# A new stored table of places and engines for a fused attention and gated MLP kernel

## The chip, the core and the metric

The kernel runs as one program on one core of a Trainium2 chip. The metric is the device time in microseconds (us) of one execution; before the change its median is 655.58 us over 3 runs (651.97 to 656.78).

The core has five instruction queues that run side by side and wait for one another through semaphores: PE (matrix products), DVE (vector), ACT (activations), POOL (the general engine) and SP (here: issues the DMAs). Each works through its own queue strictly in order.

## The reference

```python
# attention, 8 batches x 8 heads, 576 positions, 64 wide
scores = (1/8) * q @ k.T
psi = log1p(|i - j|) / log1p(max(i, 1))
bias = relu(psi * w1 + b1) @ w2          # (576, 576, 8 heads), the same for all batches
attn = softmax(scores + bias) @ v
# gated MLP on x = heads side by side, (8, 576, 512)
gate = sigmoid(causal_conv(x, conv_w))   # 5 taps for each of 512 channels
out  = (gate * (x @ w_val)) @ w_out
```

The inputs are float32. Where the kernel multiplies in 16 bits it splits an operand into a high and a low half and adds up two or three products, and it divides by the softmax's sum only after the product with v.

## The kernel before

**The parts.** `bias_rows` (L294) builds the bias once, 16 rows of positions at a time in 36 pieces: ramps on ACT, DVE and POOL, a product on PE, then a copy to SBUF and a store to DRAM in a skewed layout, from which `bias_ld` loads it back for each pair of heads. `weight` brings the two weight matrices into 16-bit halves. `pair(n)` (L603) is attention for two heads of one batch, 32 of them; `mlp(b)` (L1096) is the gated MLP of one batch, 8 of them, whose work lies among that of the pairs after it. The MLP of the last batch has only the end of the kernel to lie in.

**One pair.** For each of four blocks of 128 rows (and a fifth, `c` = 4, of the 64 remaining rows of two pairs): `qkm` on PE makes the scores of both heads (8 products, tile t_sp, L704); `logits` on DVE adds the bias and finds the row's extreme (L750); `expo` on ACT takes the exponential (L762). In 24 of the 32 pairs ("split" pairs) the exponentials are then split: `top` casts them to 16 bits (ACT L194, POOL L198 or DVE L196), `rest` subtracts that from the original for 2 x 512 columns and `rest8` for the last 2 x 64 (POOL or DVE, L217), and `swap` transposes both halves by a DMA issued on SP (L943). The other 8 pairs normalise first (`norm`, L824 or L212) and transpose on PE (`tp`, L909, with copies `tev`). `piece` (L976) multiplies with v: five groups for each half g of the 512 rows; `rem_mm` (L1050) does the remaining rows; `ev` and `mu` (L1033, L1075) bring the result to SBUF. v itself is scaled and split by `vinv` (L658), `vhi` (L212) and `vlo` (L205).

**One MLP.** Taps of the convolution run on DVE through PSUM (L1173) or, for the last channels and the last batch, as products on ACT or POOL (`prod`, L1133, L1135) and sums on DVE or POOL (`acc`, L1138) or both in one on DVE (`conv`, L1123); `sig` is the gate on ACT (L1186). x is split into halves (`split_hi`, `split_lo`). `val` (L1241) multiplies with w_val in two parts of 256 and 320 positions and four groups d of channels, three products q each; `gf` (L1251) applies the gate on DVE; `ghi` and `glo` (L194, L196, L198 and L217) split the result; `outp` (L1307) multiplies with w_out; `ote` scales the rows out of PSUM (L1319 on ACT, L201 on DVE) and a DMA stores them.

**What sets the order.** The functions do not issue at once. Each `add(...)` makes a step (a `Task`): the engines that could run it, the function that issues it, and the steps it depends on. There are 4,041 steps. The table `ORDER` (L46 on) is the only thing that decides the sequence. Unpacked, it holds two bytes for each step, which `Plan.order` (L114) reads as step number and engine:

```python
        for lo, hi in zip(code[:n], code[n:]):
            t = self.tasks[(lo + 256 * hi) // 4]
            assert not t.done and all(d.done for d in t.deps)
            t.on, t.done = t.engines[lo % 4], True
...
    for t in plan.order():
        t.fn(t.on)
```

The steps are issued in the table's order, so each engine's queue is the table's subsequence for that engine, and buffers of the rings (4 PSUM banks for products, 2 transposed halves, 2 of q and k, 7 and 13 larger SBUF buffers) go to whoever takes them next in that order. Dependencies and the waits they need are worked out from the program as issued. The other figures in the code (due times such as `PAIR_AT`, costs in `add`) are not used when a stored table is there.

Of the kernel before, what the change touches and what calls it, by code (L numbers as in the profile page):

```python
# [1479 lines left out]
```

## Time and profile before

| | |
|---|---|
| median of 3 runs | 655.58 us (651.97 to 656.78) |
| the profiled execution | 653.45 us |
| its span, first to last instruction | 651.6 us, so 1.85 us lie outside it |
| PE busy | 617.4 us (95%), 6,176 products |
| DVE, ACT, POOL busy | 590.3, 571.9, 520.3 us (91%, 88%, 80%) |
| granted TensorE clock | 0.997 over the span |

The trace is of one execution. "Busy" is the time in which an engine has an instruction under way; the ends of PE's pipelined products are modelled, so a busy PE can still hide some waiting. The views used further on are the totals by engine, the same in four stretches of the span, the chain of work that ended last (followed back from the last instruction to what released each step), the waits, the groups of like instructions, and the timeline of single instructions.

### The profile page before, as it was taken

The page shows a single profiled execution, that of the slowest core. Times are in us where ns is not written, and L with a number is a line of the kernel's source. Part 1 is how long each engine was busy: PE and PEld are TensorE (multiplying, and loading weights), DVE is VectorE, ACT ScalarE, POOL GpSimd, SP SyncE. Part 2 cuts the span into 40 slices and gives each one's busy share as a digit, 9 for nine tenths or more (in the row PEclk, how much of TensorE's full clock was granted, in tenths as well). Part 3 has the DMA queues.
Part 4 walks back from the last instruction along what each step waited for, and adds up shares of the span by engine and source line. Part 5 has one row for each costly group of instructions (what it writes and reads, how often), then busy time and mean ns, then how long its engine had stood idle before and what let it go on. Part 6 is the DMA issues. An engine that isn't in the chain of part 4 may idle for free.

```text
span 651.6 us, 16872 instructions
## 1 busy us (share of the span) xinstructions
PE 617.4 (95%) x6176; PEld 398.0 (61%) x6176; DVE 590.3 (91%) x1575; ACT 571.9 (88%) x1284; POOL 520.3 (80%) x585
## 2 busy tenths in 40 slices
PE   6777999999899999999999999899999999999997
PEld 2223667766566666667666665666676666766663
DVE  7999999999999988898998989899989889999982
ACT  6898999999999998999789989989979998899561
POOL 5889858687797988997798989787979787898441
PEclk9989999999999999999999999999999999999999
DMA  7888885246999999999999999999964999999712
GB/s 243 274 280 283 277 307 177 82 136 126 236 160 218 207 225 207 210 199 226 206 234 225 212 230 193 211 216 198 222 162 125 179 200 195 221 201 184 133 66 81
DMA packets 279107, 129.77 MB, mean 199 GB/s; under 512 B 255600, under 2 KB 255856, under 8 KB 279024
## 3 DMA queue, kind: packets, MB, share of 16 engines
q1 hardware_dynamic: 278880, 128.40, 89.3%
q8 instruction: 48, 0.79, 0.5%
q14 instruction: 35, 0.29, 0.2%
q10 hardware_dynamic: 144, 0.29, 0.1%
HBM read 44.64 MB, written 20.33 MB: 100 GB/s over the span
## 4 chain that ended last, share of the span: by engine, by line
PE 54%; DVE 10%; POOL 10%; DMA 8%; ACT 6%; issue 3%; SPq 0%; POOLq 0%; DVEq 0%; ACTq 0%
PE t_sp L704 14%; PE t_ps L976 11%; PE t_ps L1307 9%; PE t_ps L1241 9%; DMA t_pt<-t_d 6%; POOL t_d L217 5%; PE t_ps L909 5%; DVE t_d L750 4%; ACT t_d L762 3%; DMA t_d<-t_d 2%; PE t_sp L720 2%; ACT t_d L194 2%; PE t_ps L1050 1%; PE t_ps L1029 1%; POOL t_d L198 1%
## 5 line engine op out<-in xcount | busy, mean ns | idle before, releaser
L217 POOL TENSOR_TENSOR t_d<-t_d,t_d 128x1024 f16<-128x1024 f32 (+1 forms) x180 | 245.4, 1383 | 32.8 <-ACT t_d L194 23.8
L762 ACT ACTIVATE t_d<-t_d,nm 128x576 f32<-128x576 f32 x288 | 222.2, 774 | 17.6 <-DVE nm L750 17.0
L750 DVE CUSTOM_DVE_ANT_0 t_d<-t_sp,bias 128x576 f32<-128x576 f32 x256 | 184.8, 751 | 22.7 <-PE t_sp L704 12.5
L704 PE MATMUL t_sp<-t_qk 64*128 64x288 f32 x1024 | 165.1, 429 | 1.7 <-DVE nm L750 1.2
L976 PE MATMUL t_ps<-t_pt,t_w 128*64 128x256 f16 (+1 forms) x1664 | 124.1, 296 | 7.0 <-DMA t_pt<-t_d 5.1
L704 PEld LDWEIGHTS t_sp<-t_qk 64*128 64x128 f32 x1024 | 92.6, 186 | 48.2 <-DVE nm L750 12.4
L194 ACT CAST t_d<-t_d 128x576 f16<-128x576 f32 x157 | 100.5, 668 | 7.8 <-DMA t_pt<-t_d 3.3
L1241 PEld LDWEIGHTS <-wv 128*128 128x128 f16 x768 | 72.6, 98 | 31.7 <-issue 12.4
L976 PEld LDWEIGHTS <-t_w 128*64 128x64 f16 x1344 | 69.7, 110 | 23.3 <-issue 14.0
L1241 PE MATMUL t_ps<-xh,wv 128*128 128x256 f16 (+1 forms) x480 | 69.2, 285 | 0.1
L1173 DVE SCALAR_TENSOR_TENSOR t_ps<-t_xp,convw,t_ps 128x288 f32<-128x288 f32 x126 | 64.3, 516 | 1.5 <-ACT t_ps L1164 0.8
L1307 PE MATMUL t_ps<-wo,gh 128*128 128x512 f16 x240 | 57.7, 380 | 0.0
L762 ACT ACTIVATION_READ_ACCUMULATOR t_d<-t_d,nm 128x1 f32 x288 | 56.0, 194 | 0.0
L337 PE MATMUL t_ps<-rel,w 128*32 128x272 f32 (+17 forms) x352 | 42.9, 520 | 12.2 <-ACT t_be L356 3.8
L318 POOL TENSOR_SCALAR rel<-gt,ip,nb 128x336 f32<-128x336 f32 (+14 forms) x21 | 47.1, 2248 | 8.4 <-PE t_ps L337 8.0
L824 POOL TENSOR_SCALAR t_d<-t_d,rinv 128x576 f32<-128x576 f32 x57 | 45.0, 799 | 8.9 <-DVE rinv L796 8.5
L318 DVE TENSOR_SCALAR rel<-gt,ip,nb 128x368 f32<-128x368 f32 (+17 forms) x87 | 46.5, 591 | 1.6 <-PE t_ps L337 1.6
L198 POOL TENSOR_SCALAR t_d<-t_d 128x576 f16<-128x576 f32 x49 | 35.4, 724 | 14.9 <-ACT t_d L762 7.0
L909 PE MATMUL t_ps<-ident,t_d 128*128 128x128 f32 x324 | 43.2, 278 | 0.8 <-DVE vsc L648 0.4
L909 PEld LDWEIGHTS t_ps<-ident,t_d 128*128 128x128 f32 x324 | 35.1, 140 | 14.0 <-issue 7.1
L1307 PEld LDWEIGHTS <-gh 128*128 128x128 f16 x240 | 22.1, 98 | 27.5 <-issue 4.8
L1241 PE MATMUL t_ps<-xl,wv 128*128 128x256 f16 (+1 forms) x240 | 38.0, 285 | 0.4 <-DVE xl L205 0.4
(159 smaller groups left out, 1088.6 us busy)
## 6 DMA issues: line engine op xcount, KB each, us to landing
t_qk<-qkd SPq DMA_DIRECT2D x32, 576.0 KB, 4.7
bias_d<-t_be SPq DMA_DIRECT2D x36, 295.5 KB, 4.5
bias<-bias_d SPq DMA_DIRECT2D x16, 576.0 KB, 6.5
out<-t_w SPq DMA_DIRECT2D x32, 256.0 KB, 3.0
t_w<-vd SPq DMA_DIRECT2D x24, 320.0 KB, 3.9
t_w<-vn SPq DMA_DIRECT2D x8, 320.0 KB, 4.3
t_d<-wod SPq DMA_DIRECT2D x4, 512.0 KB, 5.0
t_d<-wvd SPq DMA_DIRECT2D x4, 512.0 KB, 5.3
```

Of the source, the lines that this page charges most:

```text
L194: A.copy(out=out, in_=in_)
L217: (V if e == "V" else G).tensor_tensor(out=out, in0=in0, in1=in1, op=ALU.subtract)
L318: (G if e == "G" else V).tensor_scalar(out=rel[g].t[:, 0:w], in0=src, scalar1=sct[:, mm : mm + 1], scalar2=nb1, op0=ALU.mult, op1=ALU.max,)
L704: T.matmul(ts[a][:, j, 0:hw], lhsT=qk.t[r, c * P : (c + 1) * P], rhs=qk.t[r, x : x + hw], start=True, stop=True,)
L750: V.tensor_tensor_reduce(out=part(c, a).rearrange("p (j f) -> p j f", j=2), in0=sp.t[:, :, 0 : S // 2], in1=bias.rearrange("p (j f) -> p j ...
L762: A.activation(out=part(c, a), in_=part(c, a), func=AF.Exp, bias=nms[c][:, a : a + 1], scale=-1.0, accum_out=sums[c][:, a, 0:1],)
L824: (G if e == "G" else V).tensor_scalar(out=t, in0=t, scalar1=rinvs[c][:, a : a + 1], scalar2=1.0, op0=ALU.mult, op1=ALU.mult,)
L909: T.transpose(t[:, k * P : (k + 1) * P], es[c].t[:, (k0 + k) * P : (k0 + k + 1) * P], ident)
L976: T.matmul(po.t[r, 0:256], lhsT=vt.t[:, v, r], rhs=pt[:, x, :, :] if tr else pt[:, :, x, :], start=(t == 0 and m == 0), stop=(t == 4 and m ...
L1173: V.scalar_tensor_tensor(out=o, in0=x, scalar=wt, in1=t, op0=ALU.mult, op1=ALU.add)
L1241: T.matmul(pm.t[:, 0:w], lhsT=weights["wv"][wi][:, k, d * P : (d + 1) * P], rhs=xb.t[xi][:, k, 0:w], start=(q == 0 and k == 0), stop=(q == ...
L1307: T.matmul(pm.t, lhsT=gb.t[gi][:, k, o : o + P] if o < 256 else gx.t[gi][:, k, :], rhs=weights["wo"][wi][:, k, :], start=(q == 0 and k == ...
```

## The change

Only the lines of `ORDER` differ. Its origin is stated as a search for the mean over runs in which every step of three engines is shaken widely. The 4,041 steps, what each computes and what each depends on stay as they are. 97 steps run on another engine than before, and within each queue many steps stand a few places earlier or later. Two of the table's lines stand here, the first of the old and the first of the new:

```diff
 ORDER = (
-    'c-nPW4`?#!nfJ>#nn^NACUML+NhZl8ndBRjNgR_&GD#*|TinAv{J<?1+~O7&+`}F&xWz5*Vh?**u;3OKT(HF+F1X+p_prsUxQBbV;8*P7ci3XVf(5_g9`4~D7TjVFx7_oN`T7s;aprlSKfmYqyz}RMC&69fyoU66-4x~v(*8iG-cXuSi>on>I?LxSA6l$7d%Ica<Xfdk^!Zpkk#75J<w`Qs^LK;JK&bDqyPou9ELpErSlk&Fx`W{e52qsT'
...
+    'c-mc84`?d+oj31I%p{p4lQ<@mWRgshNix1n;+TxdB$>S0;vR1Cfm<xN#Vszlhdo?yi#=?a9u{2iz!rPBU=Q!GV8Jae*y1bh;T|ryhdq3U1q&AJ;THF>hkJNni#=?)?{9ps*WTCPpYNZ~_w)PBZ|3)#5%-8oIv?rxDijt7(~V%L9^n|4&)+<4wxnje(P`Q24rj5@ZI`35_$!G{AenJgs;O*0)N{Fm;mE-0>3_`1SW0bF1zb%JN8@PR+xNNa'
...
 )
```

By kind, the steps that change engine and that the prediction speaks of:

| step | moves |
|---|---|
| `rest8` | 9 from DVE to POOL |
| `glo` | 7 from DVE to POOL, 4 from POOL to DVE |
| `ghi` | 5 DVE to ACT, 2 ACT to DVE, 4 POOL to ACT, 3 ACT to POOL |
| `top` | 5 POOL to ACT, 1 DVE to ACT, 1 ACT to POOL, 1 ACT to DVE, 1 POOL to DVE |
| `tev` | 4 (of 512 columns) DVE to ACT, 1 (of 128) ACT to DVE |
| `ote` | 5 DVE to ACT, 3 ACT to DVE |
| `vlo`, `vhi` | 1 DVE to POOL, 1 ACT to POOL |
| `acc` | 1 POOL to DVE (in the last MLP) |
| steps of a few columns, and single others | 38 |

**First place: POOL in the last pair.** POOL's queue before, from a half for the second-last MLP to the last `rest8`. `x2x64` is a `rest8` of a pair, `rhl`, `rinvs` and `bsc` are small steps, `gh` and `gl` halves for `outp`, and L198 on a t_d a `top`:

```order
L198 TENSOR_SCALAR gh<-t_w_324 128x256
L804 TENSOR_TENSOR rhl<-rinvs,rhl 128x4
L198 TENSOR_SCALAR t_d_561<-t_d_810 128x576
L217 TENSOR_TENSOR gl<-t_w_324,gh 128x256
L217 TENSOR_TENSOR t_d_561<-t_d_810,t_d_561 128x2x64
L201 TENSOR_SCALAR bsc<-bsc 128x1
L198 TENSOR_SCALAR t_d_716<-t_d_853 128x576
L787 TENSOR_SCALAR rinvs<-sm_140 128x4
L198 TENSOR_SCALAR rhl<-rinvs 128x4
L787 TENSOR_SCALAR rinvs<-sm_140 128x4
L793 TENSOR_TENSOR rinvs<-sm_140 128x2
L217 TENSOR_TENSOR t_d_415<-t_d_200,t_d_415 128x2x64
```

And POOL's queue with the change, at the same place:

```order
L198 TENSOR_SCALAR gh<-t_w_367 128x256
L217 TENSOR_TENSOR gl<-t_w_317,gh 128x256
L217 TENSOR_TENSOR gl<-t_w_367,gh 128x256
L198 TENSOR_SCALAR t_d_197<-t_d_716 128x576
L217 TENSOR_TENSOR t_d_197<-t_d_716,t_d_197 128x2x64
L787 TENSOR_SCALAR rinvs<-sm_140 128x4
L201 TENSOR_SCALAR bsc<-bsc 128x1
L217 TENSOR_TENSOR t_d_314<-t_d_854,t_d_314 128x2x64
L787 TENSOR_SCALAR rinvs<-sm_140 128x4
L793 TENSOR_TENSOR rinvs<-sm_140 128x2
L198 TENSOR_SCALAR rhl<-rinvs 128x4
L217 TENSOR_TENSOR t_d_571<-t_d_364,t_d_571 128x2x64
```

Three `rest8` of the last pair stand in the new queue where there were two (the one from t_d_854 to t_d_314 was DVE's), and one of the two `top` casts is gone to ACT.

**Second place: DVE before the last product with v.** DVE's queue before, from the last `rest` of the last pair (L217, x2x512) to the `vlo` of its v (L205):

```order
L217 TENSOR_TENSOR t_d_415<-t_d_200,t_d_415 128x2x512
L658 RECIPROCAL vsc<-vsc 128x1
L1251 SCALAR_TENSOR_TENSOR t_w_417<-t_w_314,t_ps_169 128x320
L796 RECIPROCAL rinvs<-rinvs 128x2
L1123 SCALAR_TENSOR_TENSOR t_w_329<-t_xp,convw,t_w_329 128x576 x2
L1251 SCALAR_TENSOR_TENSOR t_w_328<-t_w_202,t_ps_191 128x320
L196 CAST gh<-t_w_416 128x256
L196 CAST gxh<-t_w_416 128x64
L205 SCALAR_TENSOR_TENSOR t_w_318<-t_w_327,vsc,t_w_318 128x640
```

And DVE's queue with the change:

```order
L1123 SCALAR_TENSOR_TENSOR t_w_199<-t_xp,convw,t_w_199 128x576
L796 RECIPROCAL rinvs<-rinvs 128x4
L217 TENSOR_TENSOR t_d_571<-t_d_364,t_d_571 128x2x512
L590 RECIPROCAL bsc<-bsc 128x1
L205 SCALAR_TENSOR_TENSOR t_w_315<-t_w_319,vsc,t_w_315 128x640
L196 CAST gh<-t_w_366 128x256
L196 CAST gxh<-t_w_366 128x64
L1123 SCALAR_TENSOR_TENSOR t_w_326<-t_xp,convw,t_w_326 128x576
```

`vlo` now follows the `rest` at once but for a small step; the taps of the convolution (L1123), the gates (L1251) and the casts of the MLPs (L196) that stood ahead of it stand behind it or further off, and the `vinv` (L658) that it needs stands before the `rest`, outside these rows.

**Third place: PE at the end.** PE's queue before, from the last product of the last MLP's 256 positions to the first product with w_out (every row stands for four products and their weight loads, and rows of the same group are left out):

```order
L1241 MATMUL t_ps_181<-xl,wv_103 128x256
...
L1241 MATMUL t_ps_186<-t_d_810,wv_103 128x320
...
L1241 MATMUL t_ps_191<-t_d_810,wv_103 128x320
...
L1241 MATMUL t_ps_191<-t_d_853,wv_103 128x320
L1307 LDWEIGHTS gh
L1307 MATMUL t_ps_169<-wo_105,gh 128x512
```

And PE's queue with the change:

```order
L1241 MATMUL t_ps_187<-xl,wv_103 128x256
L1241 LDWEIGHTS wv_103
L1241 MATMUL t_ps_192<-t_d_716,wv_103 128x320
...
L1241 MATMUL t_ps_192<-t_d_854,wv_103 128x320
L1307 LDWEIGHTS gh
L1307 MATMUL t_ps_169<-wo_105,gh 128x512
```

Two groups of 12 products for the 320 positions lay between them (t_ps_186 and t_ps_191); with the change it is one (t_ps_192), and the other has gone to before the products of the 256 positions.

## Rows read from the trace of the kernel before

**Rows 1.** The page: the four engines' busy time, share of the span, instructions.

```profile
PE 617.4 (95%) x6176; PEld 398.0 (61%) x6176; DVE 590.3 (91%) x1575; ACT 571.9 (88%) x1284; POOL 520.3 (80%) x585
```

**Rows 2.** Four stretches: length, each engine's busy time (instructions), granted clock, DMA, GB/s.

```profile
0.00:60.00 60.00, 44.25 (x358) 15.80 (x358) 53.82 (x122) 50.19 (x103) 46.94 (x38) 0.97 0.85 276
60.00:613.50 553.50, 538.85 (x5542) 360.71 (x5539) 512.40 (x1405) 506.94 (x1155) 460.57 (x532) 1.00 0.96 200
613.50:648.00 34.50, 34.31 (x282) 21.51 (x282) 24.13 (x50) 14.19 (x28) 12.76 (x16) 1.00 0.16 51
648.00:651.60 3.60, 0.00 (x0) 0.00 (x0) 0.00 (x0) 0.54 (x1) 0.00 (x0) 1.00 0.49 187
```

**Rows 3.** The page: the chain that ended last, shares of the span by engine.

```profile
PE 54%; DVE 10%; POOL 10%; DMA 8%; ACT 6%; issue 3%; SPq 0%; POOLq 0%; DVEq 0%; ACTq 0%
```

**Rows 4.** The chain in order of time: start, length, engine and line.

```profile
62.62 1.17 PE t_sp L704 x8
...
608.17 1.23 DVE t_d L217
...
609.93 0.73 DVE t_w L1123
...
612.63 0.80 DVE t_w L205
...
613.47 3.14 PE t_ps L976 x54
...
634.86 12.96 PE t_ps L1307 x60
```

**Rows 5.** The page, groups of instructions: busy, mean ns of one | idle before.

```profile
L704 PE MATMUL t_sp<-t_qk 64*128 64x288 f32 x1024 | 165.1, 429 | 1.7 <-DVE nm L750 1.2
...
L1307 PE MATMUL t_ps<-wo,gh 128*128 128x512 f16 x240 | 57.7, 380 | 0.0
```

**Rows 6.** DVE groups by shape, columns as in the rows above.

```profile
L1138 DVE TENSOR_TENSOR t_w<-t_w,t_w 128x576 f32<-128x576 f32 x18 | 15.4, 858 | 0.2
...
L217 DVE TENSOR_TENSOR gl<-t_w,gh 128x256 f16<-128x256 f32 x20 | 11.9, 594 | 0.5 <-ACT gh L194 0.4
L217 DVE TENSOR_TENSOR t_d<-t_d,t_d 128x128 f16<-128x128 f32 x20 | 8.5, 426 | 0.0
...
L196 DVE COPY t_pt<-t_ps 128x512 f32<-128x512 f32 x7 | 4.8, 686 | 1.6 <-PE t_ps L909 1.6
```

**Rows 7.** POOL groups by shape.

```profile
L217 POOL TENSOR_TENSOR t_d<-t_d,t_d 128x1024 f16<-128x1024 f32 x92 | 201.9, 2194 | 29.6 <-ACT t_d L194 20.8 <-DVE t_xp L998 3.6 <-DVE t_d L196 3.1
L217 POOL TENSOR_TENSOR t_d<-t_d,t_d 128x128 f16<-128x128 f32 x88 | 47.0, 535 | 3.1 <-ACT t_d L194 3.0
...
L198 POOL TENSOR_SCALAR t_d<-t_d 128x576 f16<-128x576 f32 x49 | 35.4, 724 | 14.9 <-ACT t_d L762 7.0 <-DMA t_pt<-t_d 2.9 <-ACT t_xp L194 2.0
L217 POOL TENSOR_TENSOR gl<-t_w,gh 128x256 f16<-128x256 f32 x40 | 28.7, 722 | 3.2 <-ACT gh L194 1.5 <-DVE rinvs L796 1.1 <-DVE gxh L196 0.3
```

**Rows 8.** ACT groups by shape.

```profile
L194 ACT CAST t_d<-t_d 128x576 f16<-128x576 f32 x157 | 100.5, 668 | 7.8 <-DMA t_pt<-t_d 3.3 <-DMA t_d<-t_d 1.9 <-POOL t_d L217 1.0
...
L194 ACT COPY t_pt<-t_ps 128x512 f32<-128x512 f32 x57 | 31.9, 593 | 1.8 <-PE t_ps L909 1.3
```

**Rows 9.** Waits of all engines: waiter, releaser: us in total, times, longest.

```profile
PE t_ps L976 <- DMA t_pt<-t_d: 5.1, 5, 1.9
```

**Rows 10.** Timeline of the last MLP: start, length, engine, line, what.

```profile
629.73 2.88 POOL L1138 TENSOR_TENSOR t_w<-t_w,t_w 128x576 f32<-128x576 f32 x2 [1.42 <-ACT t_w L1186]
...
631.44 3.42 PE L1241 MATMUL t_ps<-t_d,wv 128*128 128x320 f16 x24
...
633.24 1.01 ACT L194 CAST gh<-t_w 128x256 f16<-128x256 f32 x3
...
634.70 3.62 PE L1307 MATMUL t_ps<-wo,gh 128*128 128x512 f16 x16
```

**Rows 11.** Timeline: a `rest8` on POOL, beside the DVE row at 608.17 above.

```profile
608.21 1.47 POOL L217 TENSOR_TENSOR t_d<-t_d,t_d 128x128 f16<-128x128 f32 x1 [2.33 <-ACT t_d L194]
```

More of the change, by code (lines that the diff above doesn't have):

```diff
@@ new lines @@
+    'r|+xxKD-)FQGJ^u;Y}x3Kb=qlp<_6DXNU=+<Y(oi?JL3XXv}^!?ofF9SuLEZIWxT+N44r{JD$!y5v6Zua_<tdsMzczS%}cATr5RnL`20VF1N?)yK?AAoPrzSQf$q7xz#3`?XH{QI+aFGNqhai{-D<BR#Uw|F!YT~uAlYipS-fUV;T*^@9D5wJn61gbXYW&NhF0-HealyB~cy6CV0D4UP?p@@uXa7)N-BPkEo0%>n+hfHs>!lZA!J?w|5<k'
+    'lM4)nRabBn3V&KL4c*>At?u!?G0qExV51cZ5Yk2Qx6R0SqKm$*V(l<ab|T%XTx;4KEyeC6RO&`4S8BF87PmF<r@{Aop-pGP?yx&ujN227Pjrs3N|0(I8FBfd@cdN6sdOfnuV=s2fBTDE{h3s?RYFmlKi~;QLQU1-ipHunA3GWpV4)_7Vr)46a@ijYJ9U9j#4Uce)lSvp$wsr4=CeXh8dl}ZtFTP<W^d3@5~+N*(ASM%x{cQN{=41bG9#P>'
@@ new lines @@
+    'tBYlGMXan6Ch8ZPPw^O&Ajl3CDE9Dtuo9}2iiL3I*Pn9TQZ3ua<qKt+AS3@#SK~>Fo-nM<E?`6>RS~N=*;M<E@zCko;r97-Oh||=sV&1wDA^!3n6RUNbjOpqf}AfJJMVPUbcXGfct=_3kA{OGFOs8>AlvLN>UWNh-1UY}R9uqKY_&VxaF!`tea`N1Z#E;I7Bi0KO3qh2J-;`==8LhU`~5dl@VNK`6Nw9YeIcjN=5%2-p5WywtWKwIiFoq0'
+    '0wAJ+axfGL{Cy^?_6M+MsX@0lELKX@3BJ^RhW#cKj?gOJ<i@r7?*lok6=hgXr|^OlWq5X05JkKbi`x>;WU8B%t-+9*$^NvF%InfOJK=J;!%;R8Gm?reVJ95U&DTBNST#vz;yHh!;2z2WHIvU4L{~Po6MsKZEFHztu%0DPrCft23vOF4SS}Sq{ZYKqf$L6I37BN3M>6$NrOj6x@xhonYbIOPM0b?!p$nK~*nTosOl8x#QGVDR>k3|%4#R1N'
@@ new lines @@
+    '{euqcRp>nDE0o8ja<SXN+q@vVeQm<ejq8n0JEfo_&OKi38YeRo+|M^Xt&T74(GeI~5vmif-O&?Sr@t@3?viVRPe0CZpNPZNFx8(>UKfAv3P_u};fU~z75P3wqV*5LVL2FKgJ8&}E?6j<NraMa#-=*CVyT?YWO->=u@9vjJyN6LSUizTM-zhRc6@Cn5=qHbg^R_Lsjt7Bdbd`v+0z*t>%#D{$4^W$q&)x&M0Q49YRqCSRq*<P)f$taIfk#b'
+    '`M0vUYA+85R^eM=%R7QtYt~D3XSNdSE3)GFeFKKC)O^jB%}Lv-D&C4GzXs<==nHO7F2IH(`GMqjOHNsFxz(ucC5NX@1pI-RBN&VXWAS+08&boGO4J!jB+|)L13i<yB!&|t^$j)pkuM3;4rkKcl#fYetNl97mLsvEE1Ppw>Ts~+-1%HSUuYD2{cdy6f-RoT)Jug%yXyI2;k{x4=GLe+i@jmk+a5+@oo;KC?R48CH6BfjCte*zV+=PaluBh^'
@@ new lines @@
+    '<wLw!;@@DUa;>MU_Zu89kd!FVOorwAgE7I$$rL%!Wdp*5P;4&FUT8FPZoyM@$o|*)AO585Om~P}84lM*v-9&0D$P;L*KPNxegOOVhvRA+tKpq4J?Kr|d<)mv?4l$qO@~bo!)m)V>_*5@e|bPs_I9uHpY^K0;1rdf<mit_@?absvNh*tqlya~PW%k(<XrA?AUGIq;xC1GX7U<-9`d}b6EPPLPgort@BVNq7*V4!7(^HN>(#HPb2Vp(py*8g'
+    '`-N0IS4cNVCSgnFGsP?~cv(u6U(Mx<C0bODdBL|6m2906&M8$HZiwQwIel%`ABdvI%9WnzN|@W{_xMwGJ8Vq5Lw2UQFaK3ABz1A2-pB;PFPD=QQHsT@i4;6b&15kX4o2dwG#od*ehj7+QaxUHclbkra6B~#CerFnG80ihs%LXc<hz|x7WQs2WC=&qaxIb?cH*T<z1r|4qs2seRIYRfWwb|$UU%4s2QOC{+G%F=o9=j$AH$)G;Tgvhl3}yT'
@@ new lines @@
+    'y9F1;!g1jtDQ=P_+X*~HyIq{u&HFr|LO5E?2|8`BW=pW63Z-0;Dwpf~4R|WrxVG!cZeHL8P`Fs+Z~FOC;h!p2TU>5-S|5J<ok~5e5Hm^aSD*B&@R&7iT~X@wi^EnsTq1k+!3R`z$PQ|mQGPUVjOmx2OkUA_aX8YZNXlcvMR`P}5NcJpjw}-s$NN<&Qma=QaK>=FC@b)0BS5n;g0s`KcXY*BN2_grB#5(LVBMZ4C6W?wN!@%cnutWzZd^>X'
+    'doegs!jb4Gs>b>Q)jEzPG1yYEjx-MXhjAv6OvWcR+^r*a-brUR;ktaRz=^!X*;5`z$jM7CFG;~|PNlPUmpjkaLV>yfpAi{{+vyAXb4<wPb$V0}OwQ)|vOOFnHzPj3JMHs&{BLEd=%@|1TY(_q2t{I%SU4N+<hXJrn+aqKx@s=}F%?%aSoeILu8H9Uo-70<TPhvNOm}{_i_YHf{3MwwtG(W^UX<-!{^`Br*?2S|JpDnR996<eUpku`jJ<)l'
@@ new lines @@
+    'Q0?byiF6^FYWRZXA*^fB>6-lIS9RgYC|SwiRG{uAVzC`Il`U0^Kg;FOi)n%-S|v4^iN<v`vHZ_<I9Gmtl+NMpVR|&qlsa7!o&`7r1~|(RB+v5Cem0!cE2DScYmXC!PVv`S)9hgKJE2r<&**#@hZBKnqb%SQNl`Aet!*@y4Ki-p18*AM&I%t}i+M8S4@YT-)7vgEK2esKenhU+V*XA)UQ8rQN{Xb|f9*Azj)7Xs<>C2Ptb(i*Y;Y@R8yv)<'
+    'T@bqyIpjoNZ~kD&r{o;=mjg~g>J4qq(KsKD$ZD({jwo>3bSk`RNV+8vtlj3Nn93J0$ckcB+2?<+7LKq{#rB?$bA<d);(?+A4#{fG=~mC}F&F;M2YldfUG*<{f*C?|V6btE=rf@=Xp}1DwAxJcqp{J4ua(`Y>NuY84Ru&jls}Rtb;Tdx@m1r`1SuHu`oqD$^F;>IzkTH`)fTnGOLRESRdzOy_CNa2l$!{n%*^*%`S<W@t<glgfvEe@gIlX('
@@ new lines @@
+    'jdn&B>m)2)L#V?WTKT%z`bB@FYuegfoFKBl>h*KuKVS<^7fZTnj^h8~SDq*_5O?4ymE?OB9a61)(e-wF^_M?(cc`nhQb?9QKNx;4WA}~5&R*G7ffJzf>w()#p^fIL`-c<v>vVVId0Xc#Fuj1oSqlG;9%qTT$(AS-E17sA1slSd<;l|btLadtShh!=C0*WduGgoUtwAb6b80`$?DN9V=Wcht84UePJ=TauVM=XB7|t^I|1nY`u}s#f#w%ZX'
+    'BajZdyfsHOVRM&#9)F|R>$e8sTssete}`GYl9bYgWXj$Ryg9@(#R}{3X5;F}?F{9$^8*hNzvBwI*Td2L_j75I$D%|tQ~XXcRjQWZFTzLl7J7(T-e&ig+P(5Ku^Y-ay&hjIA}d^9jd$Q8C0nZ^B$7ct%qFFF|7$!P*|V`sJ|4>cpirDVExXEHTn_8fnP{vD?_)X}S8|UX3@5g_<4Po#NZ9OER%#EPbb5Vxg2UUp(t%6umQ%gF^VQ@lSf@J>'
@@ new lines @@
+    '(1x&MAAIDh_N#oLH}v&wwNHmQHK;n=za3BNy1}qLQqWNwigdc((O5_H8H^l<;ccZ8CSD9aaagX#v-L*rjk?f$hWiOpcDVy##beXac8+v8TJ8ya#3%V(mV1-;c>8j%O?BMe9@g}bL;FxjX>YD{4Za^5X_Xq`tqhT(YfbN<ZGnr6OFsChFJ#bLr_`$F1UZp^*8b(kuNRvl!)`LK4`23kgO(5C{!&ORSd~CHm@G<PdwB$h)@U4u?Nd)Uzwyne'
+    '(>5umlbKZZB}c~<DHK2X!MLGD1F>KTPPMQu0vjzp`LTc0S8Hm_`^9|4lPZm2r30;Qx7n^Y;7#=HfA}P-ef}`;0U}BY{ByIxcc<F}pKsAvI*4aO{bG*Dzt?P2**JU#CV`ZN^R(1Ul?Sz0<-^)DmK%=vF_27VFgQhQ@TW!WQ1;J1p$q@;<DI9k!G`{+<cBr%1Ydirn~0D;F8u71iH@W&x<5Y{G9!W=>;7D@Kh-g0WB)%gqZOoJGe~qZGnj6c'
@@ L76 @@
+    'Q|=&ocXxFsLJKZX!3N_BfLB+_?X7YJpzG)K3QX_%P67Y5a;qo`;zs!(0DZ2Y$Q_C*_mBagYc!&wh)9DVYC!;be|0xCv^>oV`m_V{ehRz(quf8%CVqW?tvtTIe-76e?(gok3%W-#ZU0PUS?eA@26gJtn#Yf2s30<m+&|XJbKGNSwfcD4zfd3lnTq84T7In2d<Mzm&wv8z<NpOgT&=P'
 )
```

39 lines of the change are left out of this document (11 added, 28 removed).

## The prediction, made before the changed kernel was run

> **What bounds the kernel now.** I read the totals by engine first, then the same totals in four stretches, then the chain that ended last, then the waits and the groups of like instructions, and the timeline only where the two queues' orders differ most.
>
> The totals say that PE is busy for 617.4 of 651.6 us and that three more engines are close behind: DVE 590.3, ACT 571.9, POOL 520.3 [rows 1]. The stretches show where PE is not busy [rows 2]. Up to 60 us, while the bias is built, it is idle for 60.00 - 44.25 = 15.75 us; there DVE is at 53.8 of 60. From 60 to 613.5 us, where attention and MLPs lie side by side, it is idle for 553.50 - 538.85 = 14.65 us. From 613.5 to 648 us, the last products, it is idle for 0.2 us, and 3.6 us follow in which the last rows are scaled and stored. The granted clock is 0.97 or more of full speed (2.4 GHz) in each stretch. So the profiled time is a sum: 617.4 busy + 15.75 + 14.65 + 0.2 + 3.6 inside the span, and 1.85 outside it, 653.45 us. That is 2.1 us under the median of the runs shown, 655.58, and inside their spread of 651.97 to 656.78; I make the sum against the profiled run.
>
> Not all of the busy time is work. A block's scores take 1.17 us where nothing is late [rows 4]; the 128 blocks take 165.1 us [rows 5], which is 165.1 - 128 x 1.17 = 15.3 us more. The products with w_out run at 12.96 us for 60 at the end [rows 4]; 240 of them at that pace take 51.8 us, and they take 57.7 [rows 5], 5.9 us more. So some 21 us of lateness hide in PE's busy time beside the 14.65 us of open idle time: about **36 us in the long middle stretch** is what another order could win. PE waits there for many things, none of them large: the biggest pair, products with v behind a transposing DMA, is 5.1 us in 5 waits [rows 9]. The chain crosses all engines, PE 54%, DVE 10%, POOL 10%, DMA 8%, ACT 6% [rows 3]. No single wait is there to be removed.
>
> **The change, part by part.** Nothing is added or removed: 4,041 steps, 6,176 products, the same transfers. What is left are four terms.
>
> *Steps that change engine.* The nine `rest8` leave DVE at 0.426 us each [rows 6] and cost POOL 0.535 [rows 7]: -3.8 and +4.8. Three `glo` net leave DVE at 0.594 and cost POOL 0.722: -1.8 and +2.2. Four copies `tev` of 512 columns leave DVE at 0.686 and cost ACT 0.593 [rows 8]: -2.7 and +2.4. Of `top`, ACT gets four more net at 0.668, +2.7, and POOL loses five at 0.724, -3.6. Together DVE -8.3, ACT +5.1, POOL +3.4; the remaining moves go both ways or are of a few columns, and I set them at nothing within the bounds. Of DVE's busy time 10% x 651.6 / 590.3 = 11% lies on the chain; of ACT's 39.1 / 571.9 = 7%; of POOL's 65.2 / 520.3 = 12.5% [rows 1, 3]. That gives -0.9 + 0.4 + 0.4 = **-0.1 us**. The ends are -8.3, if all that DVE sheds had been on the path, and +8.5, if all that the others take on is. I take the value by shares because DVE's load is spread over the whole run just as the chain is.
>
> Beside this stands what two engines do to each other. A `rest8` on POOL took 1.47 us [rows 11] in place of the usual 0.535 [rows 7], while DVE ran a `rest` from 608.17 for 1.23 us [rows 4], which reads two operands from SBUF; so a step of this kind can wait for the other engine. The Trainium skill (SBUF — State Buffer, section on the two separate sides) says that DVE with two SBUF operands and POOL take a shared port pair in turn, and that the loser waits for the whole instruction; the row above agrees, 1.47 against 0.535. By that rule the 3.4 us that POOL takes on could hold up DVE's two-operand steps for as long, and the sum would be 3.4 x 0.11 = 0.4 us larger, an estimate.
>
> *The first 60 us.* On DVE, ACT and PE only neighbours change places. On SP the bias stores change places with their neighbours and some loads for pairs that come later move too. I take **0**, with 2 us either way as bounds: about one ramp or one `rest` on POOL, 2.19 us [rows 7], is what a late neighbour costs.
>
> *The end.* Before the last products with v PE waits for `vlo`, which DVE runs from 612.63, after taps, gates and casts that follow the `rest` of 608.17 [rows 4]. In the new order `vlo` follows that `rest` almost at once, so it can end some 3 us earlier. But PE has other work there: of the 553.5 us of that stretch it can win only what it idles, and the whole gap between the chain's steps at 612.63 and 613.47 is 0.84 us. I take half, **-0.4 us**, bounds -0.8 and 0. Against that, the last products for the 320 positions now give one group of 12 as cover, 3.42 / 2 = 1.7 us, where two did [rows 10]; behind that cover the gate of the last channels, its product and the casts must be done. Before, the casts ended at 634.25 and the first product with w_out came at 634.70 [rows 10], 0.45 us to spare. One sum of the convolution goes from POOL at 1.44 us (two in 2.88) [rows 10] to DVE at 0.858 [rows 6], 0.6 earlier. So PE may stand for 1.7 - 0.45 - 0.6 = 0.65 us; I take half, **+0.3 us**, bounds 0 and 1.7.
>
> *Fillers.* In the middle PE's queue keeps its skeleton of scores and products with v; what moves are MLP products, row sums and transposes, which fill the waits, by a few places, and in each of the other queues likewise. These swaps can shorten or lengthen the 36 us. No row prices them. The nearest are the two sums above: nothing, if each wait only changes its name, and a third of the 36, 12 us, if every third wait finds a filler; the same 12 us on the other side. I take **-1.8 us**, a twentieth, because DVE, the busiest behind PE, is the one relieved.
>
> Sum: 653.45 - 0.1 + 0 - 0.4 + 0.3 - 1.8 = 651.45, say **651.5 us**, which is 0.6% under the median shown.
>
> **Rivals.** *The middle tightens.* If the new fillers take a third of the hidden and open lateness, 12 us go in place of 1.8: 651.5 - 10.2 = 641.3 us; with the relief of DVE on the path instead, -8.3, it is 643.3. For it: the lateness is spread over many small waits, which is what a new order can reach, and DVE, at 512.4 of 553.5 us in the middle [rows 2], loses work. Against: ACT at 506.9 gets more, and PE's skeleton is the same. Chance 0.22.
>
> *POOL makes the transposes late.* The nine `rest8` used to run on DVE beside POOL's `rest`; on POOL they come after it, 0.535 us later at the least, and 2.19 + 0.535 = 2.7 us later where another `rest` stands ahead [rows 7]. `swap` cannot start before, and what is queued behind it on SP starts later too. Nine times 2.7 is 24.6 us; if PE runs out of other work in half of them, 12.3 us are added: 653.45 + 12.3 = 665.8 us. It decides from the point where PE's waits for the transposes grow beyond the 5.1 us of now [rows 9] to well over 10. Against it: 88 of 108 `rest8` are on POOL already. Chance 0.13.
>
> *Nothing but names.* The moves fall beside other work and each wait is replaced by a like one: 653.5 us. That is inside my forecast's own spread.
>
> **Numbers.** The forecast, some 651.5 with 5 us to either side, has 0.65. About 1% is what a measurement of this kernel can tell from no change: 649.0 to 662.1 us around 655.58. Faster by more than that takes the first rival or the lower end of the forecast, 0.23; slower by more the second rival, 0.12; in between 0.65. The range runs from 643, where the first rival lies, to 660: it takes in the bound of the two ends and start (+1.7, +2) and part of the second rival, and leaves out the rest of both.
>
> **What would show it.** If I am right, PE stays busy for 615 to 619 us and its idle time from 60 us to the last products is 11 to 15 us; DVE's busy time falls by 8 to 12 us and ACT's rises by 5 or more; `vlo` of the last pair ends before 611 us counted in the same order of things, that is right behind the last `rest`; the products with w_out begin with under 1 us of idle. PE's wait for `t_pt` by DMA stays under 8 us. I am wrong if PE's busy time itself falls by more than 4 us (the hidden lateness went), if the first 60 us change by more than 2 us, or if the waits for transposes double.

## The result, and the profile after

The changed kernel takes 658.49 us in the median of 11 runs (656.51 to 660.70), the kernel before, run beside it, 655.34 (651.95 to 656.78): a ratio of 1.0062, 95% interval 1.0041 to 1.0083 (the means, 658.59 and 654.54 us, give this ratio; the medians alone give 1.0048). By the ratio that is 4.1 us (2.7 to 5.4) slower, where 4 us faster was forecast: inside the range of 643 to 660 us and inside 1%, outside the 5 us to either side of the forecast, and with the wrong sign.

The profiled execution took 658.85 us. Its totals by engine, which answer to [rows 1]:

```profile
span 657.1 us, 16868 instructions
PE 623.4 (95%) x6176; PEld 398.3 (61%) x6176; DVE 584.5 (89%) x1547; ACT 577.1 (88%) x1299; POOL 520.9 (79%) x599
```

PE is busy 6.0 us longer with the same 6,176 products; DVE lost 5.8 us, ACT gained 5.2, POOL 0.6. The stretches, as in [rows 2], with the last cuts put where the new kernel's last products lie:

```profile
0.00:60.00 60.00, 46.62 (x374) 15.81 (x375) 55.20 (x128) 51.87 (x107) 45.07 (x38) 0.97 0.88 281
60.00:613.50 553.50, 537.10 (x5452) 357.22 (x5450) 501.22 (x1361) 506.84 (x1156) 461.66 (x543) 1.00 0.94 197
613.50:653.00 39.50, 39.50 (x355) 25.29 (x353) 28.07 (x60) 17.74 (x37) 14.18 (x20) 1.00 0.32 83
653.00:657.10 4.10, 0.22 (x2) 0.00 (x0) 0.00 (x0) 0.69 (x1) 0.00 (x0) 0.88 0.34 104
```

In the first 60 us PE idles 13.38 us in place of 15.75, from there to 613.5 us 16.4 in place of 14.65, and at the end not at all. So open idle time hardly moved, and the extra time stands inside PE's busy time, which can hold both more work and hidden waiting. PE's waits from 60 to 620 us (what waited, for what: us in total, times, the longest), to be held against [rows 9]:

```profile
PE t_ps L976 <- DMA t_pt<-t_d: 3.8, 5, 1.6
PE t_sp L704 <- DMA t_qk<-qkd: 2.0, 2, 1.3
PE t_sp L704 <- DVE nm L750: 1.9, 4, 0.9
PE t_ps L976 <- ACT gxh L194: 1.7, 1, 1.7
PE t_ps L1307 <- DVE t_xp L1033: 1.3, 1, 1.3
PE t_ps L1241 <- DVE t_xp L1075: 1.0, 2, 0.7
```

The products with v wait less for transposes than before (3.8 for 5.1 us). New are a load of q and k that comes late (2.0) and some single waits of 1 to 2 us. No wait is large.

A timeline of PE shows what else the new order does (start, us, engine, line, operation, tiles, count):

```profile
290.03 1.24 PE L704 MATMUL t_sp<-t_qk 64*128 64x288 f32 x8
291.21 1.04 PE L1307 MATMUL t_ps<-wo,gl 128*128 128x512 f16 x4
292.17 0.41 PE L976 MATMUL t_ps<-t_pt,t_w 128*64 128x256 f16 x4
292.51 1.90 PE L1307 MATMUL t_ps<-wo,gh 128*128 128x512 f16 x8
```

The figure behind the tiles (128\*128, 128\*64, 64\*128) is the part of the array that the product uses. A group of four products with v (128\*64) stands alone between MLP products (128\*128). Sorted by that figure, PE's steps are of three kinds: MLP products and PE's transposes over 128 by 128, products with v and their row sums over 128 by 64, scores with 64 rows (the bias products of the start, 128 by 32, are a kind of their own). Counted along PE's queue, neighbours of unlike kind are **332 in the old table and 357 in the new** (331 and 356 in the rows of the two traces, the same 25 more); the difference is that of the direct contacts of the first two kinds, 42 before and 67 now, while those of the scores with the two shift by 7 against each other. That a contact costs something can be read in the trace of before, at the four sets of value products of one group and the scores behind them (L720 here is the line of the fifth block's scores):

```profile
377.59 0.61 PE L1241 MATMUL t_ps<-xh,wv 128*128 128x256 f16 x4
378.04 0.60 PE L1241 MATMUL t_ps<-xl,wv 128*128 128x256 f16 x4
378.48 0.60 PE L1241 MATMUL t_ps<-xh,wv 128*128 128x256 f16 x4
378.91 0.60 PE L1241 MATMUL t_ps<-xl,wv 128*128 128x256 f16 x4
379.44 1.73 PE L720 MATMUL t_sp<-t_qk 64*64 64x288 f32 x16
```

Each set starts 0.43 to 0.45 us after the one ahead; the scores, of another kind, start 0.53 us after the last set, 0.09 later than one more set would. In the changed kernel's trace four output products with their own kind behind them take 0.86 us from start to start:

```profile
613.06 1.03 PE L1307 MATMUL t_ps<-wo,gh 128*128 128x512 f16 x4
613.92 1.03 PE L1307 MATMUL t_ps<-wo,gl 128*128 128x512 f16 x4
```

The four of 291.21 above, with products with v behind them, take 0.96. The experiments below ask whether that is the cause.

### The profile page after: what moved, and what is told of

Same layout as the page of the kernel before. It is cut to its first block, busy times and chain, and to the rows that moved or that the text cites. A ratio compares the mean times of both kernels' runs of the same rounds, so it can differ in the third digit from the quotient of the medians.

```text
span 657.1 us, 16868 instructions
## 1 busy us (share of the span) xinstructions
PE 623.4 (95%) x6176; PEld 398.3 (61%) x6176; DVE 584.5 (89%) x1547; ACT 577.1 (88%) x1299; POOL 520.9 (79%) x599
## 4 chain that ended last, share of the span: by engine, by line
PE 60%; DMA 9%; POOL 8%; DVE 7%; ACT 5%; issue 3%; SPq 0%; POOLq 0%; DVEq 0%; ACTq 0%
PE t_sp L704 14%; PE t_ps L976 13%; PE t_ps L1307 12%; PE t_ps L1241 10%; DMA t_pt<-t_d 7%; POOL t_d L217 5%; PE t_ps L909 5%; DVE t_d L750 3%; PE t_sp L720 2%; ACT t_d L762 2%; PE t_ps L1050 2%; PE t_ps L1029 1%; ACT t_d L194 1%; DVE wv L553 1%; DMA biasr<-bias_d 1%
## 5 line engine op out<-in xcount | busy, mean ns | idle before, releaser
L217 POOL TENSOR_TENSOR t_d<-t_d,t_d 128x1024 f16<-128x1024 f32 (+1 forms) x189 | 250.9, 1346 | 31.7 <-ACT t_d L194 22.4
L750 DVE CUSTOM_DVE_ANT_0 t_d<-t_sp,bias 128x576 f32<-128x576 f32 x256 | 185.1, 751 | 29.9 <-PE t_sp L704 20.7
L704 PE MATMUL t_sp<-t_qk 64*128 64x288 f32 x1024 | 167.9, 429 | 4.1 <-DMA t_qk<-qkd 2.0
L976 PE MATMUL t_ps<-t_pt,t_w 128*64 128x256 f16 (+1 forms) x1664 | 123.9, 296 | 7.1 <-DMA t_pt<-t_d 3.8
L704 PEld LDWEIGHTS t_sp<-t_qk 64*128 64x128 f32 x1024 | 94.7, 186 | 50.7 <-issue 11.7
L194 ACT CAST t_d<-t_d 128x576 f16<-128x576 f32 x161 | 102.9, 664 | 8.5 <-DMA t_pt<-t_d 7.2
L1241 PEld LDWEIGHTS <-wv 128*128 128x128 f16 x768 | 72.5, 98 | 31.9 <-issue 13.0
L976 PEld LDWEIGHTS <-t_w 128*64 128x64 f16 x1344 | 69.8, 110 | 21.9 <-issue 12.0
L1241 PE MATMUL t_ps<-xh,wv 128*128 128x256 f16 (+1 forms) x480 | 68.5, 286 | 1.2 <-DVE t_xp L1075 1.0
L1307 PE MATMUL t_ps<-wo,gh 128*128 128x512 f16 x240 | 57.7, 380 | 1.3 <-DVE t_xp L1033 1.3
L318 POOL TENSOR_SCALAR rel<-gt,ip,nb 128x336 f32<-128x336 f32 (+14 forms) x21 | 44.4, 2122 | 10.2 <-PE t_ps L337 9.8
L824 POOL TENSOR_SCALAR t_d<-t_d,rinv 128x576 f32<-128x576 f32 x56 | 43.5, 787 | 11.3 <-DVE rinv L796 10.8
L337 PE MATMUL t_ps<-rel,w 128*32 128x272 f32 (+17 forms) x352 | 44.6, 513 | 8.3 <-ACT t_be L356 3.2
L198 POOL TENSOR_SCALAR t_d<-t_d 128x576 f16<-128x576 f32 x44 | 31.2, 713 | 12.6 <-ACT t_d L762 7.1
L194 ACT COPY t_pt<-t_ps 128x512 f32<-128x512 f32 (+1 forms) x84 | 37.4, 497 | 3.8 <-PE t_ps L909 3.4
L212 ACT ACTIVATE t_xp<-t_ps,vsc 128x256 f32<-128x256 f32 (+1 forms) x72 | 29.5, 412 | 11.6 <-PE t_ps L1029 4.0
```

The costliest lines, as they stand in the source:

```text
L194: A.copy(out=out, in_=in_)
L217: (V if e == "V" else G).tensor_tensor(out=out, in0=in0, in1=in1, op=ALU.subtract)
L318: (G if e == "G" else V).tensor_scalar(out=rel[g].t[:, 0:w], in0=src, scalar1=sct[:, mm : mm + 1], scalar2=nb1, op0=ALU.mult, op1=ALU.max,)
L337: T.matmul(pb[32 * g : 32 * g + 32, 0 : y - x], lhsT=w28, rhs=rel[g].t[:, x:y], start=True, stop=True, tile_position=(0, 32 * g),)
L704: T.matmul(ts[a][:, j, 0:hw], lhsT=qk.t[r, c * P : (c + 1) * P], rhs=qk.t[r, x : x + hw], start=True, stop=True,)
L750: V.tensor_tensor_reduce(out=part(c, a).rearrange("p (j f) -> p j f", j=2), in0=sp.t[:, :, 0 : S // 2], in1=bias.rearrange("p (j f) -> p j ...
```

## The experiments

Ratios are to the kernel before, run beside it on the same chip, with their 95% interval. Where a kernel's table is printed on more lines, its line numbers are 16 higher (L720 for the scores' L704, L992 for L976, L840 for L824, L233 for L217).

**Sequence and engines apart.** Two kernels, each with one half of the change:

```diff
 first: the old sequence of all steps
-the old engine for 97 steps
+the new engine for these 97 steps
 second: the old engine for these 97 steps
-the old sequence of all steps
+the new sequence of all steps
```

> The old sequence of the 4,041 steps with the new choice of engine for the 97 steps that change it: DVE loses some 6 us of work, ACT gains some 5. Theory 'sequence' (the 3.1 us are lost by the new order of the queues, the moved steps cost nothing): 655.3 us, ratio to the kernel before 1.000, within 0.2%. Theory 'engines' (ACT and POOL carry the moved steps on the path): 658.5 us, ratio 1.005 or more. If DVE's relief is a gain by itself, 653 us or less, ratio 0.997.

> The new sequence with the old choice of engine for the 97 steps. Theory 'sequence': 658.5 us, ratio 1.005 (if DVE's relief was a gain by itself, more: 660 us, 1.008). Theory 'engines': 655.3 us, ratio 1.000.

Measured: the moves alone 668.57 us, ratio 1.0219 (1.0188 to 1.0250); the sequence alone 675.14 us, 1.0310 (1.0278 to 1.0342). Both theories fall: each half costs several times what the whole costs. The sequence was fitted to these engines and the engines to this sequence. Most of the loss of the first lies in one stretch of its trace. Its scores of pair 24 start at 467.9 us (467.1 before), those of pair 28 at 542.4 (529.8 before). PE's waits from 484 us on begin with

```profile
PE t_ps L925 <- POOL t_d L840: 4.5, 1, 4.5
```

and POOL's timeline shows the step that PE's transpose waits for, a division by the row sum (`norm`, L840) that came from DVE and now stands behind a `rest` (L233):

```profile
512.54 0.67 POOL L214 TENSOR_SCALAR t_d<-t_d 128x576 f16<-128x576 f32 x1
513.29 2.12 POOL L233 TENSOR_TENSOR t_d<-t_d,t_d 128x1024 f16<-128x1024 f32 x1
515.40 0.75 POOL L840 TENSOR_SCALAR t_d<-t_d,rinv 128x576 f32<-128x576 f32 x1
```

**One step given back.**

```diff
 the old sequence, the new engines
-norm, pair 24, block 3, second half: POOL
+norm, pair 24, block 3, second half: DVE
```

> The old sequence with the new choice of engines, as in the run that took 668.6 us, but with one step given back to DVE: the second half of norm of pair 24, block 3, which had gone to POOL behind a rest and on which a transpose on PE waited 4.5 us. Theory 'one late step at a full POOL': the loss between 490 and 516 us goes with its consequences, 7 us or more of the 14.6, 654 to 661 us. Theory 'the 97 moves cost a little everywhere': 668 us.

Measured: 662.77 us, 1.0127 (1.0091 to 1.0163). The wait of 4.5 us is gone, and one step of 97 takes 0.9% with it, 6 us of 14.3. That is a little under the 7 us foreseen, and the 8 us that stay have no place found for them. POOL's next `rest8` is done at 515.1 us in place of 523.0:

```profile
511.46 2.14 POOL L233 TENSOR_TENSOR t_d<-t_d,t_d 128x1024 f16<-128x1024 f32 x1
513.85 0.74 POOL L803 TENSOR_SCALAR rinvs<-sm 128x4 f32<-128x4 f32 x1 [0.25 <-ACT t_d L778]
514.67 0.43 POOL L233 TENSOR_TENSOR t_d<-t_d,t_d 128x128 f16<-128x128 f32 x1
```

So the mechanism of the second rival, a step late behind POOL's `rest` (a `norm` here, a `rest8` there), is real; the new sequence avoids it.

**The start.** Tables that change over at about 75 us:

```diff
 third:  +the new table for 442 steps, then the old one for the rest
 fourth: +the old table for 432 steps, then the new one for the rest
```

> The new table for its first 442 steps (to about 75 us), then the old sequence and engines for all steps that are left. In the trace PE had lost 2.2 us less by then with the new table. Theory 'two parts' (the start's gain is real and lasts, the rest of the new table loses some 5 to 7 us): 653.1 us, ratio 0.9966. Theory 'given back' (what follows is not ready sooner because the start is, so the gain goes within some 80 us): 655.3 us, ratio 1.000.

> The old table for its first 432 steps (to about 75 us), then the new sequence and engines. Theory 'two parts': 658.5 + 2.2 = 660.7 us, ratio 1.008 or more. Theory 'given back': as the changed kernel, 658.5 us, ratio 1.005.

Measured: 654.20 us, 0.9996 (0.9969 to 1.0022), and 659.36 us, 1.0088 (1.0058 to 1.0118). The first speaks for "given back", the second does not exclude either. The traces agree with the first: with the new start PE idles 13.3 to 14.0 us of the first 60, with the old start 15.2 to 15.8 (seven traces each), but the first scores of pair 3 come at 94.7 to 96.0 us with the new start and at 94.7 to 96.1 with the old, in the same traces. The start's 2 us are gone by then, and the loss lies behind it.

**The old table in one stretch.**

```diff
 the new table up to 365 us
-the new table from 365 to 480 us
+the old sequence and engines for the steps of that stretch
 the new table for the rest
```

> The new table up to 365 us, the old sequence and engines for the steps that are left up to 480 us, then the new table again. In the traces the new table loses 2.5 to 3.5 us between 365 and 480 us. Theory 'the loss lies at a few places': 655.5 us, ratio to the kernel before 1.001, within 0.3%. Theory 'it is spread or follows from what went before': 658.5 us or more, ratio 1.005 or more.

Measured: 656.58 us, 1.0030 (1.0011 to 1.0049), between the two theories: half of the loss comes back, though the intervals of the two ratios allow nearly any part of it. This table has 352 changes of kind.

**SP's queue.** The transposing DMAs stand close on SP between 160 and 480 us, so I first took that queue for the bound. Two kernels with the new table:

```diff
-                        SP.dma_start(out[b, t0 + o : t0 + o + P, :], ot.t)
+                        A.dma_start(out[b, t0 + o : t0 + o + P, :], ot.t)
```

```diff
-            SP.dma_start(new(qk, [P, 2 * S], F32), qkd[b, p])
+            t = new(qk, [P, 2 * S], F32)
+            SP.dma_start(t[:, 0:S], qkd[b, p][:, 0:S])
+            SP.dma_start(t[:, S : 2 * S], qkd[b, p][:, S : 2 * S])
 (and the loads of v in two parts likewise)
```

> The changed kernel, but the stores of the output are issued by ACT and no longer by SP; the table is the new one. In the changed kernel's trace SP's queue is full from 160 to 480 us (0.87 to 1.00 of each 40 us), and 66 of the 81 transposing DMAs of that stretch had their input ready more than 0.3 us before SP came to them. Some 20 of the 36 stores lie there, 0.57 us each with their gap of 0.07. Theory 'SP's queue sets the pace there': up to 12 us of SP's time go, and the time falls by 4 or more, to 654 us or less, ratio to the kernel before 0.998 or less. Theory 'the fillers on PE, DVE, ACT and POOL are what is late': SP's relief gives nothing and ACT has 36 issues more, 658.5 to 661 us, ratio 1.005 to 1.009.

> The changed kernel with each of the 32 loads of q and k and each of the 32 loads of v issued as two halves: the same bytes, 64 more issues on SP at some 0.45 to 0.6 us. 36 of them lie in the stretch from 150 to 484 us, 16 to 22 us of SP's time. Theory 'SP's queue sets the pace there': the time rises by 8 to 20 us, to 666 to 678 us. Theory 'fillers': SP's idle time and the early issue of loads take it up, within 2 us of the changed kernel, 657 to 661 us.

Measured: 672.37 us, 1.0272 (1.0233 to 1.0310), and 664.65 us, 1.0152 (1.0122 to 1.0181). More work on SP costs: against the changed kernel 0.9% or 6 us for 64 issues, between the 8 or more of the one theory and the 2 of the other. Less work gained nothing up to there: the scores of pair 16 start at 346.9 us with the stores on ACT and at 347.0 without. Then one store whose rows come from DVE stops ACT's queue (ACT's waits from 340 to 400 us):

```profile
ACT t_d L762 <- DVE t_w L201: 8.8, 1, 8.8
```

So SP is close to a bound, but up to there it is not what the new table lost by; the rest of that run is no clean test.

**Changes of kind on PE.** The table of before with 18 pairs of neighbours on PE exchanged, each where the first two kinds meet, such as

```diff
 PE's queue: rowsum(v), MLP value
-products with v, products with v | value, value
+products with v, value | products with v, value
```

> The old table with 18 pairs of neighbours on PE exchanged where a stretch of 128-row products and transposes meets a stretch of products with v, so that the two kinds alternate: on PE 368 changes between the three kinds of array use (128 by 128, 128 by 64, 64 rows) in place of 332; each exchanged step moves by under 1 us and no other queue changes. Theory 'each change of kind costs PE 0.2 to 0.3 us' (read from the traces: a value product of 256 columns takes 0.436 us before one of its kind and 0.636 us before another): 36 x 0.21 = 7.6 us more, 662 to 664 us, ratio 1.0115. Theory 'late steps' (what counts is which step waits for which): 655.3 us, ratio 1.000 within 0.3%.

Measured: 657.19 us, 1.0048 (1.0026 to 1.0071), 3.1 us (1.7 to 4.6) for 36 changes. The sign is that of the theory; "late steps", 1.000, lies outside the interval. The price is 0.09 us for one and not 0.21. I had read it from the step ahead of a change alone (0.436 us between weight loads before its own kind, 0.636 before another) and had overlooked that the step behind a change is shorter (0.344): 0.20 - 0.09 = 0.11.

**Fewer changes.** Blocks of PE steps moved by at most 2 us (3.5 in the last) beside their own kind, first in the new table, then twice in the old:

```diff
-357 changes (new table)      332 changes (old table)
+325, 28 blocks moved         306, 20 blocks    296, 28 blocks up to 3.5 us
```

> The new table with 28 small blocks of PE steps moved by at most 2 us to stand beside their own kind: 325 changes of kind in place of 357; the other queues and the engines as in the new table. Theory 'changes of kind': 32 x 0.21 = 6.7 us less than the changed kernel, 651 to 653 us, ratio to the kernel before 0.995, thus below it. Theory 'late steps': 658.5 us or more, ratio 1.005.

> The old table with 20 small blocks of PE steps moved by at most 2 us to stand beside their own kind: 306 changes of kind in place of 332. Theory 'changes of kind': 26 x 0.21 = 5.5 us less, 650 us, ratio 0.992. Theory 'late steps': 655.3 us or more, ratio 1.000.

> The old table with 28 small blocks of PE steps moved by at most 3.5 us: 296 changes of kind in place of 332. Theory 'changes of kind': 36 x 0.21 = 7.6 us less, 648 us, ratio 0.9885, if the farther moves make nothing late; each that does gives a part back, 648 to 653 us. Theory 'late steps': 655.3 us or more, ratio 1.000 or more.

Measured: 669.06 us, 1.0227 (1.0202 to 1.0253); 669.56 us, 1.0253 (1.0214 to 1.0293); 682.84 us, 1.0450 (1.0411 to 1.0488). All three are misses: what changes of kind give is 3 to 4 us at 0.11, and what the moved blocks make late is four to eight times that. In neither table do two blocks of scores follow each other on PE; in these they do at 2, 6 and 8 places, and the second finds no free bank. In the second kernel PE's wait for DVE's release of the scores' banks is 6.5 us, 1.2 before, and the scores are busy 176.8 us and idle 7.2 ahead of them, 165.1 and 1.7 before: 17.2 us more, nearly all of what its moved blocks cost.

```profile
L720 PE MATMUL t_sp<-t_qk 64*128 64x288 f32 x1024 | 176.8, 433 | 7.2 <-DVE nm L766 6.5 <-DMA t_qk<-qkd 0.4
...
PE t_sp L720 <- DVE nm L766: 6.5, 9, 1.1
...
407.68 1.24 PE L720 MATMUL t_sp<-t_qk 64*128 64x288 f32 x8
409.88 1.91 PE L720 MATMUL t_sp<-t_qk 64*128 64x288 f32 x8 [0.96 <-DVE nm L766]
411.72 1.90 PE L1323 MATMUL t_ps<-wo,gh 128*128 128x512 f16 x8
```

The eight output products of 411.72 stood between the two before. Such runs cannot price a change of kind, since they move steps.

**A change of kind by itself.** Two kernels with the old table and no step moved. At the head of each of the 100 groups of MLP products stand two added products of 64 columns, whose result the group's first product overwrites; they differ in the second alone:

```diff
                     if q == 0:
                         bank(pm)
+                        w0, x0 = weights["wv"][0], xb.t[0][:, 0, 0:64]
+                        T.matmul(pm.t[:, 0:64], lhsT=w0[:, 0, d * P : (d + 1) * P], rhs=x0, start=True, stop=True)
+                        T.matmul(pm.t[0:P, 0:64], lhsT=w0[:, 0, d * P : d * P + P], rhs=x0, start=True, stop=True)
 (in the other kernel pm.t[0:64, 0:64] and d * P : d * P + 64; in outp likewise)
```

> The kernel before with two more products of 64 columns at the head of each of the 100 groups of MLP products (64 of value, 36 of output), both over the whole array as the products behind them; the group's first real product then starts the bank anew, so the output is the same. It is the measure for the next run: 200 more products at some 0.06 to 0.11 us, 12 to 22 us more than the kernel before, 667 to 677 us, by every theory.

> As the run before it, but the second of the two added products is of the other kind, 128 rows by 64 columns of the array, in each of the 100 groups: 200 more changes of kind, with every step in its place. Theory 'each change of kind costs PE 0.2 to 0.3 us': 40 to 60 us more than the run with two products of the same kind. If as much of it as in the run with 36 more changes is taken back by waits that shrink (3.1 us measured, 0.09 us each): 18 us more. Theory 'late steps': within 3 us of that run.

Measured: 657.48 us, 1.0053 (1.0031 to 1.0074), and 676.31 us, 1.0338 (1.0294 to 1.0382). The same 200 products cost 3.5 us over the kernel before when they are of the group's kind, far less than foreseen, and 18.8 us more with 200 changes of kind: 0.094 us for one. That is the figure foreseen for the price of the run with 36 changes, and far from the 3 us of "late steps". PE is busy 624.1 us in the one and 643.1 in the other. One group in each, L1240 and L1241 being the added products:

```profile
380.71 0.20 PE L1240 MATMUL t_ps<-xh,wv 128*128 128x64 f16 x1
380.75 0.19 PE L1241 MATMUL t_ps<-xh,wv 128*128 128x64 f16 x1
380.78 0.60 PE L1244 MATMUL t_ps<-xh,wv 128*128 128x256 f16 x4
381.21 0.60 PE L1244 MATMUL t_ps<-xl,wv 128*128 128x256 f16 x4
```

```profile
387.45 0.20 PE L1240 MATMUL t_ps<-xh,wv 128*128 128x64 f16 x1
387.58 0.22 PE L1241 MATMUL t_ps<-xh,wv 128*64 128x64 f16 x1
387.73 0.61 PE L1244 MATMUL t_ps<-xh,wv 128*128 128x256 f16 x4
388.18 0.60 PE L1244 MATMUL t_ps<-xl,wv 128*128 128x256 f16 x4
```

From the first added product to the first real one it is 0.07 us in the first kernel and 0.28 in the second: 0.21 us for two changes, with no wait in either. The busy time of a row (0.19 and 0.22) hides it; the starts show it. The Trainium skill (TensorEngine Tiling (Array Packing), section Key Properties) says that a change of the tiling mode drains TensorE; these rows agree in that a change costs time, and put it at 0.1 us here; what PE does in that time they do not show.

## Why the prediction was wrong

*The step that failed is the fillers.* It took -1.8 us for swaps on PE and the other queues, because DVE is relieved, and said that no row prices them. As start and end came to nothing, this term and the moved steps together measured +4.1 us (2.7 to 5.4), where -1.9 was forecast. One part of it has a price that could be read beforehand: 25 more changes of kind. At the 0.11 us of the trace that is 2.7 us, at the 0.09 of the timed runs 2.3. This is the price in the old table, times a count; no run here takes the 25 changes out of the new table and leaves its steps in place. The rest, some 1.5 us with 0 inside its uncertainty, is lateness. In the two traces, one execution each, it stands at the scores, where the changed kernel has

```profile
L704 PE MATMUL t_sp<-t_qk 64*128 64x288 f32 x1024 | 167.9, 429 | 4.1 <-DMA t_qk<-qkd 2.0 <-DVE nm L750 1.9
```

against 165.1 busy and 1.7 idle in [rows 5]: 5.2 us more, 2.8 of them inside PE's busy time. With 2.3 us for the changes of kind and the 2.4 us that PE idles less in the first 60 us, that makes 5.1 of the 5.5 us by which the two spans differ. Some of the 5.2 is only the start's gain given back: the kernel with the new start and the old rest, as fast as the one before, has 168.0 busy and 3.0 idle there. Which wait the rest goes back to was not settled; the late load of q and k is one candidate, and the run with the old table from 365 to 480 us gives back more (0.3%, 2 us) than its 5 changes fewer explain, so some of it may lie there. The relief of DVE came to 5.8 us and bought nothing: DVE's wait for the scores on PE ahead of the logits grew instead, from 12.5 us in the profile before to 20.7 (before, then after: busy, mean ns | idle before, releasers):

```profile
L750 DVE CUSTOM_DVE_ANT_0 t_d<-t_sp,bias 128x576 f32<-128x576 f32 x256 | 184.8, 751 | 22.7 <-PE t_sp L704 12.5
L750 DVE CUSTOM_DVE_ANT_0 t_d<-t_sp,bias 128x576 f32<-128x576 f32 x256 | 185.1, 751 | 29.9 <-PE t_sp L704 20.7
```

*The 36 us of lateness* stood in the prediction as what another order could win, with 12 us either way as ends. Of these, the 21 us that hide in PE's busy time were misread. The 1.17 us of a block and the 12.96 us of 60 output products are times from start to start, and the busy time of a group runs to the end of its last product, behind the start of the next group. A block with nothing late is busy for 1.24 us (the row at 290.03 above): 128 of them make 158.7 of the 165.1 us, so 6.4 are late, not 15.3. The output products of that group stand in 19 runs of eight at 1.90 us (292.51), 14 of four at 1.03 (613.06) and two of sixteen at 3.62 [rows 10], which makes the whole 57.7 us, with nothing late. So some 6 us hid in these two groups, and what an order could win by fewer waits was, by them, nearer to 21 us than to 36. The ends of 12 us held here, but not for an order that does not fit: the regrouped tables lose 15 to 29 us. What was missing is that an order also sets how much work PE has, and not only when it waits: 332 changes of kind at 0.09 us are some 30 us of PE's time, an estimate.

*Steps that change engine.* Foreseen were DVE -8.3, ACT +5.1, POOL +3.4; it is -5.8, +5.2, +0.6, so the moves set at nothing, and means that differ between the two executions, made 2.5 us on DVE and -2.8 on POOL. The price by shares of the chain, -0.1 us with ends of -8.3 and +8.5, cannot be a price: the same moves cost 14.3 us in the old sequence (ratio 1.0219), and in the new one they gain 16 (1.0310 without them, 1.0062 with them), both outside those ends. Whether a step can move is decided by what stands ahead of it on the new engine at that moment. The two engines' hold on each other did not grow to matter: a `rest8` on POOL takes 0.554 us in the mean of 97, 0.535 before; the 0.4 us that the prediction estimated for it is too small for any run here to show.

*The first 60 us.* Taken at 0; PE idles 2.4 us less there, but the gain is gone at pair 3, and the new start with the old rest measures 0.9996. The 0 was right in its effect, though the prediction named a change of over 2 us as a sign of error.

*The end.* From 613.5 to 653 us PE has no idle time, so neither `vlo` nor the thinner cover of the last products cost anything; +0.3 and -0.4 cancel to next to nothing, which is what came. That the time lies in the range at all is owed to its upper end at 660, put there for the second rival and the bounds of start and end, none of which came; that part is luck.

*The rivals.* "The middle tightens" did not come. "POOL makes the transposes late" is refuted for this change: PE's wait for the transposed halves fell from 5.1 to 3.8 us. It is what happened to the moves without the sequence. "Nothing but names", 653.5 us, was nearest among the cases, and wrong for the reason above.

*What would show it.* PE busy 615 to 619 us: it is 623.4, and only its fall stood there as a warning. By itself it does not point to the changes of kind: the moves in the old sequence, with not one change of kind more than before, have PE busy 623.5 us. PE's idle time from 60 us to the last products, 11 to 15 us foreseen, is 16.4; DVE's fall, 8 to 12 us foreseen, is 5.8. The signs that held, PE's wait for the transposes under 8 us and ACT's 5 us more, say nothing on the sign of the change.

## What to carry to other kernels

Where a change reorders a product queue, count the neighbours that use unlike parts of the array, before and after, and price one such contact from the starts in the timeline (here 0.1 us), since busy time does not show it. A choice of engines and a sequence are one fit: half of such a change can be far worse than the whole, so it can't be priced step by step with average shares. And fewer contacts are worth having only where no step moves that keeps two waiting ones apart: three tables with up to 36 fewer contacts were 2 to 4.5% slower than the kernel before. When lateness inside busy time is to be sized, hold a group's busy time against the busy time of one that waited for nothing, not against a time from start to start.
